# First B and C of a chunked scan: rows of 2048 bytes, turned on VectorE

## The chip, the cores and the metric

The kernel runs on one core of one Trainium2 chip. The metric is the device time of one execution in microseconds (us): three runs of the kernel before gave 373.04, 373.81 and 375.49, median 373.81.

## The reference

A gated state-space scan is followed by a gated feed-forward network. With 4 batches, 8 heads, 768 positions, head size 32, state size 16:

```python
for c in range(nc):                       # chunks; state is carried
    L = np.exp(cum[:, :, :, None] - cum[:, :, None, :]) * causal
    M = np.einsum('bhin,bhjn->bhij', Cc, Bc) * L
    y[:, :, sl] = M @ xc + (Cc @ state) * np.exp(cum)
    state = decay_full * state + sum_j(decay_from_j * Bc_j (x) xc_j)
x = y.transpose(0, 2, 1, 3).reshape(3072, 256)
out = (sigmoid(x @ w_gate) * (x @ w_val)) @ w_out      # d_ff = 1536
```

B and C are `[4, 8, 768, 16]` in memory, so the 16 values of one position of one head are 64 contiguous bytes, and 32 positions in a row are 2048.

## The kernel before, in words

The sequence is cut in 6 chunks of 128 positions, and each chunk in two halves of 64. A *unit* is one chunk of one batch (4 units a chunk, worked in pairs). For a unit TensorE transposes B and C (tile `pt`), ScalarE copies them out (`bct`), TensorE multiplies them (`pcb`), VectorE weighs that with the decays (`m`, line 478; the decays are scans, lines 419 and 586), and TensorE multiplies with x and adds the state (lines 490, 497, 541 or 624). The finished 128 positions x 4 batches are 512 columns of the network: gate and value (`pg`, `pv`, twelve pieces f = 0 to 11), then the projection (`po`, lines 839 and 850).

Chunk 0 is special. Its "unit" holds the first 64 positions of two batches (units 0 and 1, *first pair*) or the second 64 (units 2 and 3, *late pair*). Its decays come from matmuls `pa` (line 580) and scans (586). Its network starts as soon as the first pair is done: pieces f = 0 to 3 are run in halves (line 714; first halves need the first pair's result in `xw`, second halves the late pair's). Weights of the network are loaded as 512 KB pieces `wr` and taken apart in place by a chain of five steps (lines 318, 323, 325, 329, 331: VectorE, ScalarE, VectorE, ScalarE, GpSimd).

The order on every engine is fixed before the run: `run()` plays all tasks against a table of costs and writes each engine's program in the order that results. `DUES` overrides the due times of single tasks, `FIRST` orders the first loads, and constants such as `free` say when an engine is taken to be free. A load occupies one of 8 completion lanes; the load eight places later waits for that one to land. All loads go through SyncE's queue.

`load_first` (line 271) brings chunk 0's B, C and x in two DMAs of 64 partitions for each half, with positions on partitions: rows of 64 bytes for B and C, 128 for x. `products` (377) has two transposes for a unit, then an eviction by three ScalarE instructions, then 8 matmuls. `first_results` (604), `first_outputs` (629) and `first_states` (638) finish a pair. `spread` (572) makes the decays. The clipping of the whole `a` (903), its running product (912) and their way through memory (924, 927, 283, 291) give the later chunks their decays.

Of the kernel before, what the change touches and what calls it, by code (L numbers as in the profile page):

```python
# [8 lines left out]
F32 = mybir.dt.float32  # L9
# [8 lines left out]
DUES = {  # L18
# [13 lines left out]
}  # L32
WARM = 3


FIRST = "b0 c0 w0 x0 w1 b1 c1 w2 x1 w3 r w4 w5 w6 w7 w8 w9"
LANES = 8
# [30 lines left out]
def tile_ssd_then_gated_ffn(  # L68
# [16 lines left out]
    P = 128  # L85
# [90 lines left out]
    def step(eng, cost, needs=(), makes=(), port=False, **buffers):  # L176

        return eng, cost, needs, makes, port, buffers

    def run():  # L180

        free = {"sp": 1.0, "pe": 1.2 + 1.7 * WARM, "act": 3.5, "dve": 6.0, "pool": 6.2, "none": 0.0}
        port_free = [0.0]
        dma_free = 0.0
        landed = [0.0] * LANES
# [65 lines left out]
    def pair_of(tag, c, b, shape):  # L251

        k = tag, c, b // 2
        if k not in got:
            got[k] = ld.tile([P, 2, H, shape], F32, tag=tag, name=f"{tag}{c}_{b // 2}", bufs=2)
        return got[k]
# [13 lines left out]

    def load_first(tag, src, late, n):
        t = pair_of(tag, 0, 2 * late, n)
        for i in range(2):
            nc.sync.dma_start(  # L274
                t[i * L2 : (i + 1) * L2].rearrange("p u h n -> p (u h) n"),
                src[late * L2 : (late + 1) * L2, 2 * i * H : 2 * (i + 1) * H],
            )

    def load_a(c, b):
# [89 lines left out]
    class Unit:  # L369
# [7 lines left out]
        def products(self):  # L377

            c, b, u = self.c, self.b, self.u
            needs = [("bc", u)] if c else [("bc", u), ("b0", u // 2)]  # L380
            if c:
                needs += [("bct", u - 1 if c > 1 else -1), ("cb", u - 4), ("cd", u - 4)]
            yield step("pe", 0.24 if c else 0.45, needs, [("tp", u)], y=1)
# [4 lines left out]
            yield step("act", 0.9 if c else 1.1, [], [("bct", u)], y=-1)  # L388
            if c:
                self.bct = wk.tile([P, 4, L], F32, tag="bct", name=f"bct{self.nm}", bufs=4)  # L390
            else:

                if ("bct", b // 2) not in got:
                    got["bct", b // 2] = hp.tile([P, 2, 4, L], F32, tag=f"h{5 + b // 2}", name=f"bct{self.nm}")
                self.bct = got["bct", b // 2][:, b % 2]
            if u > 1:
                nc.scalar.copy(self.bct[:, :2].rearrange("p k l -> p (k l)"), pt[:, : 2 * L])
            else:
                nc.scalar.copy(self.bct[:, 0], pt[:, :L])
# [169 lines left out]
    class FirstUnit(Unit):  # L569


        def spread(self):

            u = self.u
            yield step("pe", 1.0, [("a0",)], banks=1)
            pa = ps_mm.tile([P, 512], F32, tag="mm", name=f"pa{u}")
            rows = slice(32 * (u // 2), 32 * (u // 2) + 32)
            for i in range(2):
                b = 2 * i + u % 2
                nc.tensor.matmul(  # L580
                    pa[i * L2 : (i + 1) * L2], of_b2[rows, b : b + 1].broadcast_to([32, L2]),
                    apart[rows].rearrange("p h l -> p (h l)"), start=True, stop=True,
                )
# [45 lines left out]
    def first_outputs(late):  # L629

        for i in range(2):
            yield step("act", ACT_HALF, [("inter" if late else "y", 2 * late + 1)], [("xf", late)] if i else [])
# [3 lines left out]
            nc.scalar.copy(out, got["py", late][:, i, :, 0])  # L636

# [307 lines left out]
    def initial():  # L945
# [16 lines left out]
    }  # L962
    for late in range(2):
        for tag, src, n, needs, makes in (
            ("b", b4, N, [], [("b0", late)]),
            ("c", c4, N, [], [("bc", 2 * late), ("bc", 2 * late + 1)]),
            ("x", x4, D, [], [("xn", 2 * late), ("xn", 2 * late + 1)]),
        ):
            loads[f"{tag}{late}"] = load(
                2, 1.9 if tag == "x" else 1.5, needs, makes, lambda a=(f"{tag}n", src, late, n): load_first(*a)  # L970
            )
    for i in range(NW):
# [8 lines left out]
    def unit(due, c, b):  # L981
# [9 lines left out]
        if c or b > 1:  # L991
            task(due, f"before{u.nm}", u.before())
        task(due - (0.0 if c else 30.0), f"products{u.nm}", u.products())
        task(due, f"decays{u.nm}", u.decays())
        if c == 0 and b % 2:
            task(due, f"result{u.nm}", first_results(pair.pop(), u))
            task(due, f"outputs{u.nm}", first_outputs(b // 2))
# [71 lines left out]
```

## Time and profile before

| what | us |
|---|---|
| runs shown, median (lowest to highest) | 373.81 (373.04 to 375.49) |
| the profiled execution, its own time | 374.85 |
| span of its trace | 373.0 |
| TensorE busy in the span | 360.9 (97%) |
| VectorE, ScalarE, GpSimd busy | 157.0, 151.1, 150.1 |
| TensorE busy in the first 31.62 | 24.89 |

In the trace PE is TensorE's matmuls, DVE VectorE, ACT ScalarE, POOL GpSimd, SPq the DMA issues of SyncE. [...] An idle time stands in brackets with what ended it; `issue` means that nothing in the profile shows what the engine waited for.

### The profile page before, as it was taken

What the parts mean: (1) busy time and instruction counts of PE and PEld (TensorE: products, weight loads), DVE (VectorE), ACT (ScalarE), POOL (GpSimd) and SP (SyncE); (2) the same over time, 40 slices, a digit from 0 to 9 for tenths busy, and PEclk for the clock granted to TensorE, in tenths of its full rate; (3) what the DMA queues carried; (4) which work ended last, traced back from release to release, by engine and by line L of the source; (5) the groups of instructions that cost most, each with busy time, mean ns of one, the idle gap of its engine ahead of it and who ended that gap; (6) DMA issues with size and microseconds to landing.
All of it is one profiled execution on the core that took longest, in us unless ns stands there. A gap on an engine that the chain in (4) does not pass through costs nothing.

```text
span 373.0 us, 8123 instructions
## 1 busy us (share of the span) xinstructions
PE 360.9 (97%) x3376; PEld 287.0 (77%) x3376; DVE 157.0 (42%) x277; ACT 151.1 (41%) x314; POOL 150.1 (40%) x159
## 2 busy tenths in 40 slices
PE   7788999999999999999999999999999999999996
PEld 2267668877878888888878888788877788888885
DVE  4756557768435444553354622430224440222201
ACT  2656686423575411544511245430254420254400
POOL 4425476463797520244440045430144420145410
PEclk9669999999999999999999999999999999999999
DMA  6999996527236322502332300400000000000000
GB/s 121 208 233 184 243 314 169 96 44 122 67 30 113 30 71 60 106 22 34 26 99 82 89 4 6 53 10 29 30 1 2 2 2 28 30 0 0 2 28 28
DMA packets 89270, 26.27 MB, mean 70 GB/s; under 512 B 76306, under 2 KB 82002, under 8 KB 89234
## 3 DMA queue, kind: packets, MB, share of 16 engines
q1 hardware_dynamic: 89234, 25.76, 31.8%
q8 instruction: 26, 0.43, 0.5%
q14 instruction: 10, 0.08, 0.1%
HBM read 22.41 MB, written 3.34 MB: 69 GB/s over the span
## 4 chain that ended last, share of the span: by engine, by line
PE 88%; SPq 5%; DMA 4%; POOL 1%; issue 1%; DVE 0%; ACT 0%
PE pv L813 25%; PE pg L813 24%; PE po L850 15%; PE po L851 7%; PE po L839 6%; DMA cn<-in_C_dram 2%; SPq L304 2%; PE pcb L464 2%; PE pcb L490 2%; PE pcb L541 2%; SPq L262 1%; DMA bn<-in_B_dram 1%; SPq L274 1%; PE pcb L497 1%; POOL wr L331 1%; PE pt L386 1%
## 5 line engine op out<-in xcount | busy, mean ns | idle before, releaser
L781 POOL TENSOR_TENSOR h<-g,h 128x512 fp32r<-128x512 f32 x60 | 78.5, 1308 | 126.6 <-ACT h L779 126.3
L813 PE MATMUL pv<-xh,w 128*128 128x512 f32 x264 | 93.9, 396 | 0.0
L813 PE MATMUL pg<-xh,w 128*128 128x512 f32 x264 | 93.3, 394 | 0.0
L850 PE MATMUL po<-w,h 128*128 128x512 f32 x228 | 82.1, 402 | 0.0
L775 DVE TENSOR_TENSOR g<-pv,g 128x512 f32<-128x512 f32 x60 | 41.5, 691 | 93.0 <-PE pv L813 87.5
L779 ACT CAST h<-g 128x512 fp32r<-128x512 f32 x59 | 36.6, 621 | 75.7 <-DVE g L775 75.7
L851 PE MATMUL po<-w,h 128*128 128x256 f32 x228 | 63.9, 280 | 0.0
L813 PEld LDWEIGHTS pg<-xh,w 128*128 128x128 f32 x264 | 49.6, 188 | 10.8 <-issue 0.2
L813 PEld LDWEIGHTS pv<-xh,w 128*128 128x128 f32 x264 | 49.6, 188 | 10.7 <-issue 0.3
L813 PE MATMUL pv<-xl,w 128*128 128x512 f32 x132 | 51.5, 390 | 0.0
L813 PE MATMUL pg<-xl,w 128*128 128x512 f32 x132 | 51.4, 390 | 0.0
L850 PEld LDWEIGHTS po<-w,h 128*128 128x128 f32 x228 | 42.8, 188 | 11.0 <-issue 0.5
L754 ACT ACTIVATE g<-pg 128x512 f32<-128x512 f32 x68 | 40.7, 599 | 14.7 <-PE pg L813 13.8
L851 PEld LDWEIGHTS po<-w,h 128*128 128x128 f32 x228 | 43.0, 189 | 0.2
L866 ACT COPY o<-po 128x256 f32<-128x256 f32 x20 | 7.5, 373 | 65.7 <-PE po L851 65.1
L419 DVE TENSOR_TENSOR_SCAN ab<-ab,delta 128x512 f32<-128x512 f32 x20 | 28.0, 1406 | 8.3 <-DMA ab<-a_z 8.2
L868 DVE TENSOR_TENSOR o<-po,o 128x256 f32<-128x256 f32 x20 | 8.4, 424 | 49.6 <-ACT o L866 49.5
L813 PEld LDWEIGHTS pg<-xl,w 128*128 128x128 f32 x132 | 24.8, 188 | 4.8
L813 PEld LDWEIGHTS pv<-xl,w 128*128 128x128 f32 x132 | 24.8, 188 | 4.6
L348 POOL TENSOR_TENSOR w<-wr,w 128x512 fp32r<-128x512 f32 x18 | 23.8, 1326 | 9.7 <-ACT w L346 8.8
L331 POOL TENSOR_TENSOR wr<-wr 128x512 int32<-128x512 int32 x18 | 19.6, 1091 | 20.0 <-ACT wr L329 17.9
L839 PE MATMUL po<-wr,h 128*128 128x256 f32 x96 | 23.4, 393 | 0.0
(96 smaller groups left out, 371.1 us busy)
## 6 DMA issues: line engine op xcount, KB each, us to landing
ab<-a_z SPq DMA_DIRECT2D x40, 128.0 KB
wr<-in_moe_w_val_dram SPq DMA_DIRECT2D x6, 512.0 KB
wr<-in_moe_w_gate_dram SPq DMA_DIRECT2D x6, 512.0 KB
wr<-in_moe_w_out_dram SPq DMA_DIRECT2D x6, 512.0 KB
out_dram<-o SPq DMA_DIRECT2D x24, 128.0 KB
xn<-in_x_dram SPq DMA_DIRECT2D x10, 256.0 KB
bn<-in_B_dram SPq DMA_DIRECT2D x10, 128.0 KB
cn<-in_C_dram SPq DMA_DIRECT2D x10, 128.0 KB
```

The source lines that it names most:

```text
L331: nc.gpsimd.tensor_tensor(out=lw.bitcast(I32), in0=hw.bitcast(I32), in1=lw.bitcast(I32), op=ALU.add)
L348: engines[eng].tensor_tensor(out=lo, in0=lw, in1=hi.bitcast(F32), op=ALU.subtract)
L419: nc.vector.tensor_tensor_scan(out=t.rearrange("p h l -> p (h l)"), data0=t.rearrange("p h l -> p (h l)"), data1=delta.rearrange("p h l -> ...
L754: nc.scalar.activation(gs[k, f], pm, AF.Sigmoid)
L775: nc.vector.tensor_tensor(out=g, in0=pm, in1=g, op=ALU.mult)
L779: copies[eng](hh, g)
L781: engines[eng].tensor_tensor(out=hl, in0=g, in1=hh.bitcast(F32), op=ALU.subtract)
L813: nc.tensor.matmul(pm, w[:, part, kt, fs], xx[:, kt], start=(i == 0), stop=(i == 3 * NK - 1))
L839: nc.tensor.matmul(acc[:, :DM], hs[k, f][:, js], whole[NF + f // 2][:, f % 2], start=start, stop=stop, skip_group_check=True,)
L850: nc.tensor.matmul(acc, hh, w.rearrange("p i m -> p (i m)"), start=start, stop=False, skip_group_check=True)
L851: nc.tensor.matmul(acc[:, :DM], hl, w[:, 0, :], start=False, stop=stop, skip_group_check=True)
L868: nc.vector.tensor_tensor(out=o, in0=acc[:, DM:], in1=o, op=ALU.add)
```

## The change

Five things are different in the program:

1. B and C of chunk 0 come as `rows`: 32 partitions x 2048 bytes in each of 4 DMAs (line 289 of the new kernel), and one VectorE instruction for each of B and C (line 297, `STREAM_TRANSPOSE`, 128x512) turns blocks of 32 by 32 so that positions lie on partitions as before.
2. C's rows and the first half of x are issued by ScalarE, ahead of its table load; the rest stays on SyncE.
3. `first_pair` takes the place of `products` in chunk 0: four transposes into one tile, one eviction of three wider instructions for both units, then 8 matmuls for each unit.
4. The `pa` matmuls and scans of units 2 and 3 wait for the first pair (`("cb", 1)`, `("mult", 1)`), and the second copy of `first_outputs` may go to VectorE.
5. `DUES`, `FIRST` and the start times in `free` have other numbers, which moves work of all stages.

```diff
-FIRST = "b0 c0 w0 x0 w1 b1 c1 w2 x1 w3 r w4 w5 w6 w7 w8 w9"
+FIRST = "b0 w0 w1 x1 w2 w3 r w4 w5 w6 w7 w8 w9"
+TURN = 0.6
...
-        free = {"sp": 1.0, "pe": 1.2 + 1.7 * WARM, "act": 3.5, "dve": 6.0, "pool": 6.2, "none": 0.0}
+        free = {"sp": 1.0, "pe": 0.6 + 1.7 * WARM, "act": 5.4, "dve": 5.4, "pool": 6.3, "none": 0.0}
...
+    def load_rows(queue, j):
+        if "rows" not in got:
+            got["rows"] = hp.tile([P, 2, 32, N], F32, tag="s0", name="rows")
+        src = (Bm, Cm)[j].rearrange("(i u) h (c o q t) n -> i c q (u h) o (t n)", u=2, o=2, q=2, t=32)
+        for i in range(2):
+            for q in range(2):
+                p = i * L2 + q * 32
+                queue.dma_start(got["rows"][p : p + 32, j].rearrange("p t n -> p (t n)"), src[i, 0, q])
+    def turn(j):
...
+        nc.vector.transpose(
+            got[tag].rearrange("p o u h n -> p n (u h) o"), got["rows"][:, j].rearrange("p t n -> p n t"),
+        )
...
+    def first_pair(*two):
...
+        for k in range(2):
+            for j, tag in enumerate(("bn", "cn")):
+                at = (2 * k + j) * L
+                nc.tensor.transpose(pt[:, at : at + L], got[tag, 0, late][:, k].rearrange("p h n -> p (h n)"), eye)
...
+        nc.scalar.copy(bct[:, :, :many], from_pt[:, :, :many])
+        for g in range(NG):
+            nc.scalar.mul(bct[:, :, 2 + g], from_pt[:, :, 1], of_g[:, g : g + 1])
...
-            yield step("pe", 1.0, [("a0",)], banks=1)
+            yield step("pe", 1.0, [("cb", 1)] if u > 1 else [("a0",)], banks=1)
...
-            yield step("dve", 1.22, [], [("scan", u)], banks=-1)
+            yield step("dve", 1.22, [("mult", 1)] if u > 1 else [], [("scan", u)], banks=-1)
...
+    load_rows(nc.scalar, 1)
+    load_first(nc.scalar, 0)
     nc.scalar.activation(table, table, AF.Sigmoid)
```

**The first loads.** SyncE's rows before (`cn_0`, `bn_0`: C and B of the first half; `cn_1`, `bn_1`: of the second; `DMAHW` is a completion lane):

```order
L883 DMA a_109<-in_a_dram 64x1x128
L274 DMA cn_0_121<-in_C_dram 64x16x16 x2
L304 DMA wr_124<-in_moe_w_val_dram 128x2x512
L274 DMA bn_0_126<-in_B_dram 64x16x16 x2
L304 DMA wr_129<-in_moe_w_val_dram 128x2x512
L274 DMA cn_1_131<-in_C_dram 64x16x16
L274 DMA cn_1_131<-in_C_dram 64x16x16 [waits DMAHW0_49]
```

and SyncE's now:

```order
L917 DMA a_109<-in_a_dram 64x1x128
L326 DMA wr_129<-in_moe_w_gate_dram 128x2x512
L289 DMA rows<-in_B_dram 32x1x512 x2
L289 DMA rows<-in_B_dram 32x1x512 [waits DMAHW1_49]
L289 DMA rows<-in_B_dram 32x1x512 [waits DMAHW2_49]
L326 DMA wr_135<-in_moe_w_val_dram 128x2x512 [waits DMAHW4_49]
```

B's third piece waits for lane 1, which is that of `a`, and its fourth for lane 2, which is that of the first weight. C's four pieces and x are ScalarE's.

**VectorE ahead of the first weighing** (`m_0`, `m_1` of the first pair), now:

```order
L340 TENSOR_SCALAR wr_129<-wr_129 128x512 [waits DMAHW2_49]
L297 STREAM_TRANSPOSE cn<-rows 128x16x16x2 [waits DMAHW4_49,DMAHW6_49,DMAHW3_49,DMAHW0_49]
L297 STREAM_TRANSPOSE bn<-rows 128x16x16x2 [waits DMAHW5_49,DMAHW7_49,DMAHW2_49,DMAHW1_49]
L704 SCALAR_TENSOR_TENSOR ap_161<-early 32x64 [waits Pool_49]
L592 SCALAR_TENSOR_TENSOR ab_0_163<-pa_144,delta 128x512 [waits PE_49]
L340 TENSOR_SCALAR wr_135<-wr_135 128x512 [waits DMAHW4_49]
L592 SCALAR_TENSOR_TENSOR ab_1_182<-pa_156,delta 128x512 [waits PE_49]
L340 TENSOR_SCALAR wr_137<-wr_137 128x512 [waits DMAHW5_49]
L340 TENSOR_SCALAR wr_139<-wr_139 128x512 [waits DMAHW6_49]
L347 TENSOR_SCALAR wr_135<-wt_188 128x512 [waits Activation_49]
L484 TENSOR_TENSOR m_0_225<-pcb_0_190,ab_0_163 128x512 [waits PE_49]
```

Before, all four scans stood ahead of `m_0`; now two do, and the two turns and more weight steps.

**TensorE around the late pair.** Before (`pg_f_i`, `pv_f_i`: piece f, half i of the network; lines 490 and 497 are the pair's products):

```order
L714 MATMUL pv_1_0_368<-xw_308,wr_124 128x256
L490 MATMUL pcb_2_330<-m_2_354,xn_1_222 32x64 [waits DMAHW3_49,DVE_49]
...
L624 MATMUL pcb_2_330<-cd_3_317,m_0_312 64x64 x4
L714 MATMUL pg_2_0_462<-xw_308,wr_203 128x256 [waits DMAHW1_49,Pool_49]
L714 MATMUL pg_2_0_462<-xw_308,wr_203 128x256
L714 MATMUL pv_2_0_471<-xw_308,wr_129 128x256 [waits DMAHW6_49,DVE_49]
L714 MATMUL pv_2_0_471<-xw_308,wr_129 128x256
L714 MATMUL pg_3_0_482<-xw_308,wr_203 128x256 [waits DVE_49]
L714 MATMUL pg_3_0_482<-xw_308,wr_203 128x256
```

and now:

```order
L748 MATMUL pg_2_0_376<-xw_303,wr_129 128x256 [waits DMAHW2_49,DVE_49,Pool_49]
L748 MATMUL pg_2_0_376<-xw_303,wr_129 128x256
L748 MATMUL pv_2_0_381<-xw_303,wr_152 128x256 [waits DMAHW1_49,Activation_49,Pool_49]
L748 MATMUL pv_2_0_381<-xw_303,wr_152 128x256
L496 MATMUL pcb_1_326<-m_2_344,xn 32x64 [waits DMAHW2_49]
...
L655 MATMUL pcb_1_326<-cd_3_296,m_0_308 64x64 x4
L748 MATMUL pg_3_0_472<-xw_303,wr_129 128x256 [waits Activation_49]
L748 MATMUL pg_3_0_472<-xw_303,wr_129 128x256
```

`pg_2_0` and `pv_2_0` have moved from behind the late pair to ahead of it; `pg_3_0` now follows the pair directly.

## Rows read from the trace of the kernel before

**Rows 1.** The page: queue of instruction DMA (packets, MB, share of 16 engines).

```profile
q8 instruction: 26, 0.43, 0.5%
```

**Rows 2.** Busy time by stretch (start:end, engines with instruction counts, clock, DMA share, GB/s).

```profile
0.00:31.62 31.62, 24.89 (x346) 14.06 (x346) 18.12 (x43) 15.00 (x35) 12.01 (x23) 0.78 0.89 197
27.45:29.20 1.75, 1.75 (x130) 1.59 (x129) 0.53 (x2) 0.78 (x2) 1.04 (x1) 1.00 1.02 393
60.00:370.00 310.00, 309.74 (x2897) 253.74 (x2895) 122.93 (x208) 114.77 (x235) 119.11 (x118) 1.00 0.21 43
```

**Rows 3.** The same view by half microseconds.

```profile
3.50:4.00 0.50, 0.50 (x2) 0.18 (x1) 0.00 (x0) 0.00 (x0) 0.00 (x0) 1.00 1.10 103
11.00:11.50 0.50, 0.50 (x8) 0.23 (x4) 0.50 (x1) 0.00 (x0) 0.50 (x1) 0.96 1.01 55
25.00:25.50 0.50, 0.50 (x4) 0.45 (x3) 0.21 (x2) 0.00 (x0) 0.32 (x1) 0.88 0.21 29
```

**Rows 4.** Timeline of PE (start, duration, records; idle time before and its end).

```profile
11.47 1.97 PE L580 MATMUL pa<-apart,of_b 32*64 32x512 f32 x4
15.85 0.45 PE L386 MATMUL pt<-eye,bn 128*128 128x128 f32 x1 [1.58 <-DMA bn<-in_B_dram]
18.12 0.68 PE L490 MATMUL pcb<-m,xn 64*32 64x64 f32 x32
21.18 2.05 PE L714 MATMUL pg<-xw,wr 128*128 128x256 f32 x4 [1.44 <-issue]
29.20 1.14 PE L714 MATMUL pg<-xw,wr 128*128 128x256 f32 x4
31.04 0.59 PE L714 MATMUL pg<-xw,wr 128*128 128x256 f32 x2
33.12 0.71 PE L714 MATMUL pg<-xw,wr 128*128 128x256 f32 x2 [1.50 <-issue]
45.98 0.33 PE L387 MATMUL pt<-eye,cn 128*128 128x128 f32 x1 [0.61 <-DMA cn<-in_C_dram]
70.99 0.46 PE L490 MATMUL pcb<-m,xn 64*32 64x64 f32 x32
```

**Rows 5.** Timeline of SyncE's DMA issues.

```profile
0.74 0.71 SPq L883 DMA_DIRECT2D a<-in_a_dram  x1
2.93 0.71 SPq L304 DMA_DIRECT2D wr<-in_moe_w_val_dram  x1
50.41 0.41 SPq L927 DMA_DIRECT2D a_p<-a  x1
```

**Rows 6.** Timeline of DVE.

```profile
4.30 0.22 DVE L889 TENSOR_SCALAR ac<-a 64x128 f32<-64x128 f32 x1 [2.04 <-DMA a<-in_a_dram]
7.61 0.43 DVE L318 TENSOR_SCALAR wr<-wr 128x512 f32<-128x512 f32 x1 [2.25 <-DMA wr<-in_moe_w_val_dram]
15.04 1.22 DVE L586 TENSOR_TENSOR_SCAN ab<-pa,delta 128x512 f32<-128x512 f32 x1
17.30 0.68 DVE L478 TENSOR_TENSOR m<-pcb,ab 128x512 f32<-128x512 f32 x1
42.41 1.74 DVE L912 TENSOR_TENSOR_SCAN a<-a,a 32x768 f32<-32x768 f32 x1
54.55 0.68 DVE L771 TENSOR_TENSOR h<-pv,g 128x512 f32<-128x512 f32 x1
67.00 0.69 DVE L478 TENSOR_TENSOR m<-pcb,ab 128x512 f32<-128x512 f32 x1
```

**Rows 7.** Timeline of ACT.

```profile
16.55 0.37 ACT L397 COPY bct<-pt 128x256 f32<-128x256 f32 x1 [0.69 <-PE pt L387]
```

**Rows 8.** DMA view, instruction packets in windows 22.4 to 23.9, 30.3 to 31.6, 34.5 to 35.6.

```profile
q8 instruction: 1, 0.02, 5.7%
q8 instruction: 1, 0.02, 5.9%
q8 instruction: 1, 0.02, 5.2%
```

More of the change, by code (lines that the diff above doesn't have):

```diff
@@ L254, in pair_of @@
         if k not in got:
-            got[k] = ld.tile([P, 2, H, shape], F32, tag=tag, name=f"{tag}{c}_{b // 2}", bufs=2)
+            if tag not in got:
+                got[tag] = ld.tile([P, 2, 2, H, shape], F32, tag=tag, name=tag, bufs=1)
+            got[k] = got[tag][:, b // 2]
         return got[k]
@@ L269, in load_x, with load_first @@
         nc.sync.dma_start(t[:, bs].rearrange("p b h d -> p (b h) d"), x4[cs, hs])
-    def load_first(tag, src, late, n):
-        t = pair_of(tag, 0, 2 * late, n)
+    def load_first(queue, late):
+        t = pair_of("xn", 0, 2 * late, D)
         for i in range(2):
-            nc.sync.dma_start(
+            queue.dma_start(
                 t[i * L2 : (i + 1) * L2].rearrange("p u h n -> p (u h) n"),
-                src[late * L2 : (late + 1) * L2, 2 * i * H : 2 * (i + 1) * H],
+                x4[late * L2 : (late + 1) * L2, 2 * i * H : 2 * (i + 1) * H],
             )
+    def load_rows(queue, j):
[7 more added lines that the diff above has]
+    def turn(j):
+        yield step("dve", TURN, [("rows", j)], [("b0", 0), ("b0", 1)] if j == 0 else [("bc", u) for u in range(NB)])
+        tag = ("bn", "cn")[j]
+        for late in range(2):
+            pair_of(tag, 0, 2 * late, N)
+        nc.vector.transpose(
+            got[tag].rearrange("p o u h n -> p n (u h) o"), got["rows"][:, j].rearrange("p t n -> p n t"),
+        )
     def load_a(c, b):
@@ L379, in products @@
             c, b, u = self.c, self.b, self.u
[L380 to L383, printed above, removed]
+            needs = [("bc", u), ("bct", u - 1 if c > 1 else -1), ("cb", u - 4), ("cd", u - 4)]
+            yield step("pe", 0.24, needs, [("tp", u)], y=1)
             bn, cn = (got[k, c, b // 2][:, b % 2].rearrange("p h n -> p (h n)") for k in ("bn", "cn"))
@@ L387, in products @@
             nc.tensor.transpose(pt[:, L : 2 * L], cn, eye)
[L388 to L399, printed above, removed]
+            yield step("act", 0.9, [], [("bct", u)], y=-1)
+            self.bct = wk.tile([P, 4, L], F32, tag="bct", name=f"bct{self.nm}", bufs=4)
+            nc.scalar.copy(self.bct[:, :2].rearrange("p k l -> p (k l)"), pt[:, : 2 * L])
             for g in range(NG):
@@ L602, in decays @@
             yield from self.decayed()
+    def first_pair(*two):
+        us, late = [t.u for t in two], two[0].u // 2
+        yield step("pe", 0.8, [k for u in us for k in (("bc", u), ("b0", late))], [("tp", u) for u in us], y=1)
+        pt = ps_y.tile([P, 512], F32, tag="py", name=f"pt0_{late}")
+        for k in range(2):
+            for j, tag in enumerate(("bn", "cn")):
+                at = (2 * k + j) * L
+                nc.tensor.transpose(pt[:, at : at + L], got[tag, 0, late][:, k].rearrange("p h n -> p (h n)"), eye)
+        yield step("act", 1.5 if late else 1.15, [], [("bct", u) for u in us], y=-1)
+        bct = hp.tile([P, 2, 4, L], F32, tag=f"h{5 + late}", name=f"bct0_{late}")
+        from_pt = pt.rearrange("p (u k l) -> p u k l", u=2, k=2)
+        many = 2 if late else 1
+        nc.scalar.copy(bct[:, :, :many], from_pt[:, :, :many])
+        for g in range(NG):
+            nc.scalar.mul(bct[:, :, 2 + g], from_pt[:, :, 1], of_g[:, g : g + 1])
+        for k, t in enumerate(two):
+            t.bct = bct[:, k]
+            units[t.u] = t
+        for k, (t, u) in enumerate(zip(two, us)):
+            yield step("pe", 0.3, [], [("cb", u)], **({} if k else {"cb": 1}))
+            if k == 0:
+                pcb = ps_cb.tile([P, NQ, 512], F32, tag="pcb", name=f"pcb0_{late}")
+            multiply(pcb, k, t)
     def first_results(*two):
@@ L631, in first_outputs @@
         for i in range(2):
-            yield step("act", ACT_HALF, [("inter" if late else "y", 2 * late + 1)], [("xf", late)] if i else [])
+            eng = yield step(
+                ("act", "dve") if i else "act", (ACT_HALF, DVE_HALF) if i else ACT_HALF,
+                [("inter" if late else "y", 2 * late + 1)], [("xf", late)] if i else [],
+            )
             if not xw:
@@ L635, in first_outputs @@
             out = xw[0].rearrange("p k (i u s l) -> p k i u s l", i=2, u=2, s=2)[:, :, i, :, late]
-            nc.scalar.copy(out, got["py", late][:, i, :, 0])
+            copies[eng](out, got["py", late][:, i, :, 0])
     def first_states(late):
@@ L953, in initial @@
         yield step("none", 4.9, [], [("a0",)])
+        yield step("none", 0.3, [], [("rows", 1)])
+        yield step("none", 2.8, [], [("xn", 0), ("xn", 1)])
     task(-60.0, "", initial())
@@ L962, in tile_ssd_then_gated_ffn @@
     }
[L963 to L971, printed above, removed]
+    loads["x1"] = load(2, 1.9, [], [("xn", 2), ("xn", 3)], lambda: load_first(nc.sync, 1))
+    loads["b0"] = load(4, 0.9, [], [("rows", 0)], lambda: load_rows(nc.sync, 0))
+    task(-9.5, "turn0", turn(0))
+    task(-9.4, "turn1", turn(1))
     for i in range(NW):
@@ L992, in unit @@
             task(due, f"before{u.nm}", u.before())
-        task(due - (0.0 if c else 30.0), f"products{u.nm}", u.products())
+        if c:
+            task(due, f"products{u.nm}", u.products())
         task(due, f"decays{u.nm}", u.decays())
         if c == 0 and b % 2:
+            task(due - 30.0, f"products{u.nm}", first_pair(pair[-1], u))
             task(due, f"result{u.nm}", first_results(pair.pop(), u))
```

9 lines of the change are left out of this document (2 added, 7 removed), and 25 rows, old and new, of the table DUES.

## The prediction

> **What bounds the kernel now.** I read the windows first, to find where TensorE is not full. From 60 to 370 us it is busy for 309.74 of 310.00 [rows 2], so what the change does there can only cost. Nothing but the way to a full TensorE can be shortened: in the first 31.62 us it is busy for 24.89, with 346 matmul records [rows 2], and the clock is at half in part of that [rows 3]. Next I read TensorE's timeline for the idle times that remain. Four count. At 15.85 it has waited 1.58 for B's second half; at 21.18, where the network begins, 1.44 for the first pair's result; at 33.12 it has waited 1.50 in the middle of `pg_3_0`, for nothing that a semaphore shows; at 45.98 it has waited 0.61 for C of chunk 1 [rows 4]. [...]
>
> The wait at 33.12 needs a word. TensorE had issued the first of two equal matmuls and stood before the second, which waits for nothing new. The profile has one queue of instruction packets, 26 of them [rows 1]; one lies in 30.3 to 31.6 and others in 22.4 to 23.9 and 34.5 to 35.6 [rows 8]. 3376 matmuls over 26 packets are 130 for a packet, and the late pair alone runs 130 records in 1.75 us [rows 2]. So I read this wait as TensorE running out of program: the late pair uses up one packet so fast that the next is late. This is an inference; it carries the forecast.
>
> The profiled execution took 374.85, 1.04 above the median of 373.81; I sum differences inside it and set them against the median.
>
> **First loads.** Removed are eight loads with 64-byte rows, which ran at 103 GB/s with all DMA engines busy [rows 3]. Added are eight of 2048 bytes. B is now the later of the two: its fourth piece waits until the first weight has landed. That weight took from 2.93 to 7.61 [rows 5, 6], 4.7 us, behind 64-byte rows; issued at 1.5 it lands at 6.2 by that row, or at 5.0 if the 1.2 us of 128 KB at 103 GB/s falls away. A small load takes 3.6 from issue to use (`a`, 0.74 to 4.30) [rows 5, 6]. B is whole between 8.6 and 9.8. I take 8.6, since nothing with short rows stands ahead of the weight. ScalarE's six issues and its table load end long before its first copy, and cost nothing.
>
> **The turns.** No row shows a `STREAM_TRANSPOSE`. The same 128x512 is 0.43 as one-operand work and 1.22 as a scan [rows 6]; I take 0.68, the plain two-operand row, which is nearest to one pass over one value at a time. C's turn lies before B has landed and is free; B's is on the path: VectorE is ready at 9.3, TensorE begins the four transposes there.
>
> **First pair.** VectorE's row behind the turns: `ap` (0.3), two scans (2 x 1.22), three clamps and a shift (4 x 0.43), `m_0` (0.68), two weight steps (0.86), `m_1` (0.68) [rows 6]: 6.7, so `m_1` is done at 16.0; before, it was done at 17.98. TensorE: transposes to 10.0; ScalarE's three evictions of 256 columns at 0.37 [rows 7], some 1.0, to 11.0; first products about 0.7 (32 such small records took 0.68 at half clock), four transposes about 1.3 (one takes 0.45 at half clock, and they overlap), second products 0.7, overlapping a little, to 13.4; then two `pa` at half clock, 1.97 each with some 0.2 overlapped [rows 4], to 17.1. Both engines count, TensorE is later by 1.1. x, now behind C alone and not behind two weights, has landed by then. The pair's products begin at about 16.9 in place of 18.12, and the same 3.06 (18.12 to 21.18) follow up to `pg_0_0` [rows 4]: **20.0 in place of 21.18**. With the late end for B it is 21.2, with the turn at its dear end 0.5 later still, with the cheap ends 19.5.
>
> **The clock.** [...] If the clock comes back at 25.0 again, 1.2 us gained at half rate are worth 0.6; if it comes back 3.82 after the start of the big matmuls as before (21.18 to 25.0) [rows 3, 4], 1.2. I take 0.9. [...]
>
> **The late pair.** It began at 27.45. Now `pg_2_0` and `pv_2_0` stand ahead of it, 1.84 (29.20 to 31.04) [rows 4]: 27.45 - 0.9 + 1.84 = 28.4. It runs 1.75 [rows 2], and half of `pg_3_0` takes 0.59, so TensorE stands before the second half at 30.7; before it stood there at 31.62, so 0.9 is gained so far. By the rows of the program it has then run the same 346 records. If the packet is asked for at a place in the program, it comes a fixed time after the late pair's start: 33.12 - 27.45 = 5.7 as it was; at the light end 4.0, from the third packet, which was in by 35.6, 2.5 after TensorE went on, if it is usable 1.5 after that, as the second was (in by 31.6, used at 33.12) [rows 4, 8]. That gives 32.4 to 34.1; the middle, since loads are about as dense there as before, is 33.2. **The cover that is gone** is the 1.84 of `pg_2_0` and `pv_2_0`: the gain of 0.9 turns into a longer wait, and the stage ends 0.1 later than before.
>
> **Behind it.** The wait of 0.61 for C of chunk 1 goes, since two of the chunk's transposes now come after piece 6. The weights of the network come in another order with output weights between them; the DMA engines have saved 512 KB of 64-byte rows, some 4 us, so I cost that at nothing. TensorE's work is the same. Sum: +0.1 - 0.6 = -0.5 on the profiled execution, about **373.2** on the median's scale. Ends of the forecast, from B, the clock and the packet: 372.0 to 374.5.
>
> **The rivals.**
>
> *The packet is not late* (or the 1.50 was something else). For it: no semaphore proves my reading, and `pg_3_0` is the only such place. Against it: the packet lies inside the wait's approach, 30.3 to 31.6 [rows 8]. Then TensorE goes on at 30.7, 2.4 sooner than 33.12, and with the 0.6 the time is 370.8. [...]
>
> [...]
>
> *The packet is later still*, the slower end. The loads now run without a pause from the start, eight lanes deep. If the packet's wait is that of the first one (asked for in the first pair's products at about 18.4 at the latest, in at 23.9, usable 1.5 later: 7.0), TensorE goes on at 35.4, 2.3 later than before; less 0.6, the time is 375.5. It decides from a wait of 5.3 after the late pair's start.
>
> *The decays of chunk 1 come late*. The scan of `a` ended at 44.15; now it stands behind piece 6's product, which began at 54.55, and SyncE's save at 50.41 and all decay loads stand behind the scan [rows 5, 6]. The save slips by 2 to 6 us. The second weighing was ready at 67.69; TensorE took the pair at 70.99 [rows 4, 6] and now has one more group of projection first, so some 5 us of slack. Beyond that, up to 1.5 is lost: 374.7, and more if a weight is late with it.
>
> **How the numbers follow.** Chances: forecast 0.40, packet not late 0.23, that with the clock 0.08, packet later 0.18, decays or weights late 0.11. The likeliest gives 373.2. The range leaves out the clock rival, part of "the packet is not late" below 369.7, and the worst of the last two above 375.8. A measurement tells about 1%, 3.7 us: faster than 370.07 is the clock rival and a third of "not late", 0.15; slower than 377.55 only the tail of the last two, 0.05; within, 0.80.
>
> **What would show it.** In the profile after: C's turn before B's last row, each turn near 0.68; first pair's products at about 17; `pg_0_0` near 20; half clock up to about 25; a wait of 2 to 3 us with the releaser "issue" in `pg_3_0`, behind an instruction packet, ending near 33; no wait for C of chunk 1. If `pg_3_0` runs through, the first rival was right. If TensorE waits on VectorE's weighing near 70, the decays were late. The forecast is wrong altogether if TensorE is not full from 46 on.

## The result, and the profile after

In one comparison on one chip the kernel before took 373.57 us (median of 20 executions) and the changed kernel 375.04 (20): ratio 1.0042, interval 1.0030 to 1.0054. The change makes the kernel slower, by 1.5 us, where 373.2 was forecast. The time lies inside the range (369.7 to 375.8), beyond the ends given for the forecast itself (372.0 to 374.5), and on the wrong side of the kernel before. The profiled executions tell another story than the medians: 374.56 (span 372.8) after, against 374.85 (span 373.0) before. The execution that I had read of before was one of its long ones; that of after is one of its short ones.

The first lines are TensorE's timeline of the changed kernel (start, duration, records, idle time before and its end). They answer to [rows 4].

```profile
5.97 1.93 PE L586 MATMUL pa<-apart,of_b 32*64 32x512 f32 x8
9.80 0.45 PE L618 MATMUL pt<-eye,bn 128*128 128x128 f32 x1 [1.90 <-DVE ap L704]
10.82 1.22 PE L715 MATMUL pp<-early 32*128 32x256 f32 x2
14.29 3.62 PE L586 MATMUL pa<-apart,of_b 32*64 32x512 f32 x8
17.84 0.68 PE L496 MATMUL pcb<-m,xn 64*32 64x64 f32 x32
20.79 2.05 PE L748 MATMUL pg<-xw,wr 128*128 128x256 f32 x4 [1.33 <-issue]
29.66 0.45 PE L496 MATMUL pcb<-m,xn 64*32 64x64 f32 x32
31.38 1.14 PE L748 MATMUL pg<-xw,wr 128*128 128x256 f32 x4
34.15 1.02 PE L748 MATMUL pv<-xw,wr 128*128 128x256 f32 x4 [1.63 <-issue]
```

The network starts at 20.79 in place of 21.18, a gain of 0.4 and not of 1.2. `pg_3_0` (31.38) now runs through, and the wait that nothing explains has moved one piece on, to `pv_3_0`: 1.63, until 34.15. In the profile of before `pv_3_0` started at 33.67. Behind it no wait is left, that for C of chunk 1 included. So in the two profiles the change loses 0.5 at `pv_3_0` and wins 0.7 behind it, 0.6 of that the wait for C of chunk 1.

The next are VectorE's rows; they answer to [rows 6].

```profile
3.82 0.22 DVE L925 TENSOR_SCALAR ac<-a 64x128 f32<-64x128 f32 x1 [1.56 <-DMA a<-in_a_dram]
5.90 0.47 DVE L340 TENSOR_SCALAR wr<-wr 128x512 f32<-128x512 f32 x1 [1.03 <-DMA wr<-in_moe_w_gate_dram]
7.69 1.06 DVE L297 STREAM_TRANSPOSE cn<-rows 128x512 f32<-128x512 f32 x1 [1.32 <-DMA xn<-in_x_dram]
8.65 1.01 DVE L297 STREAM_TRANSPOSE bn<-rows 128x512 f32<-128x512 f32 x1
9.56 0.23 DVE L704 TENSOR_TENSOR_SCAN ap<-early 32x64 f32<-32x64 f32 x1
15.97 0.69 DVE L484 TENSOR_TENSOR m<-pcb,ab 128x512 f32<-128x512 f32 x1
```

VectorE's first weight step starts at 5.90 (7.61 before), but a turn costs 1.0 and not 0.68, and C's turn, which I had counted as free, runs directly ahead of B's.

Then the windows (start:end, length, busy PE, PEld, DVE, ACT, POOL, clock, DMA share, GB/s), which answer to [rows 2, 3]:

```profile
0.00:31.62 31.62, 27.25 (x345) 15.03 (x346) 20.24 (x43) 13.46 (x27) 13.18 (x24) 0.73 0.92 278
8.50:9.00 0.50, 0.00 (x0) 0.00 (x0) 0.50 (x2) 0.00 (x0) 0.00 (x0) 0.78 0.97 243
9.80:20.79 10.99, 9.61 (x146) 4.83 (x147) 8.42 (x14) 6.78 (x16) 5.04 (x8) 0.50 1.08 325
25.50:26.00 0.50, 0.50 (x17) 0.27 (x17) 0.00 (x0) 0.00 (x0) 0.00 (x0) 0.65 1.05 389
46.00:60.00 14.00, 14.00 (x86) 9.85 (x86) 9.68 (x12) 9.91 (x21) 12.16 (x11) 1.00 0.24 50
```

The granted clock falls from 1.00 to 0.50 near 8.7 (0.78 in 8.50 to 9.00), while TensorE idles for the turns (1.90, up to 9.80), and is back near 25.8 (0.65 in 25.50 to 26.00); in the profile of before it was away from 11.4 to 25.0. In the same 31.62 us TensorE is busy for 27.25 in place of 24.89, for the same records: it is denser, but at a mean clock of 0.73 in place of 0.78.

### The profile page after: what moved, and what is told of

The parts are those of the page before. It is cut to its first block, busy times and chain, and to the rows that moved or that the text cites. A ratio compares the mean times of both kernels' runs of the same rounds, so it can differ in the third digit from the quotient of the medians.

```text
span 372.8 us, 8119 instructions
## 1 busy us (share of the span) xinstructions
PE 363.5 (98%) x3376; PEld 287.9 (77%) x3376; DVE 160.1 (43%) x278; ACT 150.1 (40%) x309; POOL 152.3 (41%) x159
## 4 chain that ended last, share of the span: by engine, by line
PE 95%; DMA 2%; issue 1%; DVE 1%; ACT 0%; SPq 0%; DVEq 0%
PE pg L847 25%; PE pv L847 24%; PE po L884 15%; PE po L885 7%; PE po L873 6%; PE pcb L496 2%; PE pcb L470 2%; PE pv L748 2%; PE pg L748 2%; PE pcb L547 2%; PE pcb L503 1%; DMA wr<-in_moe_w_gate_dram 1%; PE pg L838 1%; PE pv L838 1%; PE pa L586 1%; PE pt L406 1%
## 5 line engine op out<-in xcount | busy, mean ns | idle before, releaser
L847 PE MATMUL pg<-xh,w 128*128 128x512 f32 x264 | 94.8, 400 | 0.0
L353 POOL TENSOR_TENSOR wr<-wr 128x512 int32<-128x512 int32 x18 | 22.0, 1230 | 18.6 <-ACT wr L351 13.6
L425 DVE TENSOR_TENSOR_SCAN ab<-ab,delta 128x512 f32<-128x512 f32 x20 | 25.4, 1273 | 5.1 <-DMA ab<-a_z 4.8
```

Source lines behind the costliest of these rows:

```text
L353: nc.gpsimd.tensor_tensor(out=lw.bitcast(I32), in0=hw.bitcast(I32), in1=lw.bitcast(I32), op=ALU.add)
L425: nc.vector.tensor_tensor_scan(out=t.rearrange("p h l -> p (h l)"), data0=t.rearrange("p h l -> p (h l)"), data1=delta.rearrange("p h l -> ...
L847: nc.tensor.matmul(pm, w[:, part, kt, fs], xx[:, kt], start=(i == 0), stop=(i == 3 * NK - 1))
```

## The experiments

Two readings of the loss stood against each other at first. **Packet**: the wait in the middle of the network is the load of TensorE's next program packet; typical executions of before hardly have it, those of after always do. **Clock**: the change costs TensorE more time at half clock. A *record* is one matmul in the profile, and a *boundary* the record at which TensorE is taken to need the next packet. Ratios are to the kernel before, run on the same chip in the same comparison.

### Before and after again (e1, e2, e8)

No edit.

> The kernel before, unchanged, to see typical executions of it with their spans and clocks beside the profiled one (374.85, mean clock 0.982). Theory 'packet': what differs between its executions is the wait of 1.50 us in pg_3_0; most runs are then near 373.5 with the mean clock 0.982 unchanged, and a profile of such a run has no wait, or one shorter by 1 us or more, before the second half of pg_3_0, or has it at the same length where the run is 374.5 or more. Theory 'clock': what differs is how long TensorE runs at half clock; a typical run has a mean clock above 0.982 (0.984 to 0.987), and its profile shows half the clock for 10 to 12 us in place of 13.65 and the same 1.5 us wait.

> The changed kernel, unchanged. Both theories: 1.0042 times the kernel before, 374.6 to 375.3. 'Packet': its wait of 1.63 us before pv_3_0 is there in every profile. 'Clock': half clock for 17 us, mean clock 0.977, in every profile.

> The changed kernel, unchanged, beside the two below on the same chip, and for one more profile of it. 'Packet': 1.6 us of wait before pv_3_0 again, 374.3 to 375.3 where nothing else is late; an execution of 376 or more has a further wait or a longer one, with the clock as in the others. 'Loads' makes no other forecast here.

Before: 373.92 (ratio 0.9992, 0.9982 to 1.0003). After: 374.85 (1.0025, 1.0009 to 1.0042) and 375.02 (1.0033, 1.0014 to 1.0053). Of the 42 timed executions of after most lie between 374.1 and 375.8, and 11 at 375.9 to 376.4. TensorE in the second profile of before (374.08):

```profile
21.56 2.05 PE L714 MATMUL pg<-xw,wr 128*128 128x256 f32 x4 [1.44 <-issue]
28.89 0.45 PE L490 MATMUL pcb<-m,xn 64*32 64x64 f32 x32
32.48 1.41 PE L714 MATMUL pg<-xw,wr 128*128 128x256 f32 x4
33.73 1.03 PE L714 MATMUL pv<-xw,wr 128*128 128x256 f32 x4
```

`pg_3_0` shows no wait in this one, but it takes 1.41 where a piece directly behind another takes 1.03: the third of its four records comes 0.3 late, near 33.18 (an estimate: 33.73 less the 0.55 from that record to `pv_3_0` in the first profile, 33.12 to 33.67). The half clock lasted until 27.7 here (0.85 in 27.5 to 28.0), in place of 25.0 in the first profile; TensorE came to `pg_3_0` 1.4 later, and `pv_3_0` started at 33.73, against 33.67. So **clock** falls: mean clock 0.977 here, as in after, and what the clock gives back ahead of the packet the wait takes. **Packet** stands, though its forecast had the mean clock at 0.982 here. In after the wait was 1.59 in e2 (`pv_3_0` at 34.49) and 0.81 in e8 (33.79), where 1.6 was forecast.

### The gap ahead of the transposes filled (e3)

```diff
+            if u == 1:
+                for i in range(2):
+                    nc.tensor.matmul(
+                        warm.rearrange("p (r l) -> p r l", r=4), warm_sb,
+                        warm_sb.rearrange("p (r l) -> p r l", r=1).broadcast_to([P, 4, P]), start=True, stop=True,
+                    )
```

> The changed kernel with two more 128x512 matmuls of zeros ahead of the first transposes, in the 1.90 us in which TensorE waits for VectorE's turns (7.90 to 9.80). Nothing else moves. Theory 'clock': the loss is the clock that falls at 8.7, 2.7 us earlier than before, because TensorE is idle there; with the gap filled it falls at 11 to 12, the mean clock is 0.980 to 0.983 and the time 0.6 to 1.4 below that of the changed kernel, near 373.9. Theory 'packet': the two instructions hardly move the place in the program, the wait before pv_3_0 comes at a fixed time of the late pair, and the time stays within 0.4 of the changed kernel.

376.46 (1.0059, 1.0040 to 1.0078): slower, against both forecasts. Three of the six executions lie at 375.6 to 375.9 and three at 377.1 to 377.3; the profile is of the longest. The clock did stay up, to 17 (1.00 in 12.5 to 16.0), but the first pair then waited 1.74 for VectorE's weighing and began at 17.45, only 0.4 sooner; the clock fell in that wait (0.50 in 17.5 to 27.0) and was away until 27.5. The four records more moved the unexplained wait one piece up, to before `pg_3_0`, now 2.05 long, and behind it the clock fell once more (0.50 in 34.5 to 37.0). That the wait goes with the record count and not with a piece speaks for **packet**.

### The cover put back, the cover taken away (e4, e7)

The first puts `pg_2_0` and `pv_2_0` of the changed kernel behind the late pair, the second puts those of the kernel before ahead of it.

```diff
+        if (f, i) == (2, 0):
+            before += [("inter", 3)]
```

> The changed kernel with pg_2_0 and pv_2_0 behind the late pair again, as in the kernel before; the order of later work moves with them, where TensorE is full. Theory 'packet': the wait of 1.63 us is covered by the 1.84 us of these two pieces, TensorE goes on 1.0 to 1.6 us earlier, time 373.5 to 374.1 (0.996 to 0.998 of the changed kernel). Theory 'clock': half clock lasts as long as in the changed kernel (17 us), and the time stays near 375.0.

```diff
+        if late:
+            needs.append(("pv", 0, 2, 0))
```

> The kernel before with pg_2_0 and pv_2_0 ahead of the late pair, as in the changed kernel, and nothing else on purpose (the order of later work moves a little with it). 'Packet': the block between two boundaries is now the late pair alone, TensorE runs it in 1.8 us and then waits 2.0 to 2.8 us in or behind pg_3_0 in place of 0 to 1.5; it goes on at 33.8 to 35.3 in place of 33.1 to 33.4; time 0.6 to 2.0 above the kernel before. 'Loads': the packet is used at 33.2 as before, the time stays within 0.3.

381.50 (1.0195, 1.0173 to 1.0216) and 378.54 (1.0110, 1.0085 to 1.0135). Both miss: the edits moved more than they were meant to. In e4 the pair began at 27.12, 2.5 sooner, and yet TensorE stood before `pv_3_0` until 33.70:

```profile
33.29 0.62 ACT L762 ACTIVATE g<-pg 128x256 f32<-128x256 f32 x2
33.69 0.74 PEld L748 LDWEIGHTS pv<-xw,wr 128*128 128x128 f32 x4 [2.38 <-ACT g L762]
33.70 1.16 PE L748 MATMUL pv<-xw,wr 128*128 128x256 f32 x4 [1.99 <-ACT g L762]
47.40 0.33 PE L407 MATMUL pt<-eye,cn 128*128 128x128 f32 x1 [1.16 <-DMA cn<-in_C_dram]
```

By the trace this wait is one for ScalarE and not for the packet: the two sigmoids run from 33.29 for 0.62, and the weight load (PEld) ahead of the first matmul of `pv_3_0`, which in after ran at 32.14, before the wait, ran at 33.69 here. Its packet, begun in 30.3 to 31.8, took 1.4. So e4 does not test the packet. Behind 33.70 it loses 6.4 against after, to the clock behind the wait (0.50 in 35 to 37) and to waits for chunk 1. In e7 `pg_2_0` waited 1.28 for a weight that was not taken apart yet; it does not test the packet.

### The packet boundary moved (e5, e6, e9)

32 (e5, e6) or 16 (e9) small matmuls of zeros behind the second `pa` move every boundary 64 or 32 records towards the start; nothing else changes place.

```diff
+            got["pas"] = got.get("pas", 0) + 1
+            if got["pas"] == 2:
+                for i in range(32):
+                    nc.tensor.matmul(warm[:32, :32], warm_sb[:32, :32], warm_sb[:32, :32], start=True, stop=True)
```

> The changed kernel with 32 small matmuls of zeros (32x32, 64 records) ahead of the first transposes, in TensorE's idle time before 9.8. They move every packet boundary 64 records towards the start of the work: the one before pv_3_0 (record 348) goes to the middle of the late pair, and the block behind it then holds half the late pair and 18 us of the network. Theory 'packet' (a packet is asked for where TensorE enters the one before it, and is usable 4.5 us after that at the earliest; the late pair runs through a block in 3 us): no wait before pv_3_0 or anywhere else in 24 to 46, TensorE goes on at 32.5 in place of 34.2, time 1.2 to 1.8 below the changed kernel, 373.2 to 373.8. Rival 'loads' (the packet waits behind the burst of weight loads until 31.2 wherever the boundary lies, and so does something else that TensorE needs): a wait of 1 us or more stays, ending near 34, time within 0.4 of the changed kernel.

> The kernel before with the same 64 records ahead of its first transposes. 'Packet': the boundary in pg_3_0 (record 346) goes to the middle of the late pair. Executions that had no wait there (as the one of the second profile, where TensorE came to it at 33.1) gain 0 to 0.3; those that came early and waited 1.5 gain up to that, unless the wait for C of chunk 1 grows by as much: 0.995 to 1.000 of the kernel before, 372.2 to 373.9. 'Loads': as the kernel before within 0.3.

> The changed kernel with 16 in place of 32 small matmuls, 32 records, some 1.3 us, which fit the idle time ahead of the first transposes. The boundary of pv_3_0 goes 32 records up, into the last third of the late pair; the block in front of it begins at pv_0_0 or pg_1_0 and takes TensorE 7 us. 'Packet': no wait in 24 to 46, and no 1.2 us lost at the start as with 32: pg_0_0 at 20.8, pv_3_0 at 32.5 to 32.8, time 0.7 to 1.1 below that with 32 matmuls, 372.7 to 373.2. Rival: what TensorE comes earlier is lost to another wait (C of chunk 1, a weight, ScalarE's sigmoid) before 60, as in the kernel before with the shift, and the time is that with 32 matmuls within 0.3.

After with 32: 373.92 (0.9988, 0.9973 to 1.0003), none of 12 above 374.7. Before with 32: 374.91 (1.0003, 0.9984 to 1.0021). After with 16: 373.32 (0.9989, 0.9974 to 1.0004). TensorE in e5:

```profile
22.02 2.05 PE L752 MATMUL pg<-xw,wr 128*128 128x256 f32 x4 [1.33 <-issue]
32.60 1.14 PE L752 MATMUL pg<-xw,wr 128*128 128x256 f32 x4
33.58 1.03 PE L752 MATMUL pv<-xw,wr 128*128 128x256 f32 x4
```

The network starts 1.2 later than in after, and `pv_3_0` 0.6 sooner, with no wait. A kernel with useless work added is faster (0.9988 against 1.0025 to 1.0042 without), by this reading because its packets are cut elsewhere. **Packet** forecast this (with 373.2 to 373.8 a little more of it), **loads** did not. Before with the shift also loses its wait (`pv_3_0` at 32.88), but not its time, where **packet** had left room for up to 1.5 and **loads** forecast none: 0.41 of a wait for ScalarE at 54.33 is seen, and its profile (span 372.4) stands where that of e1 does (372.3). These runs together say most about the cause: moving the boundary takes after from 1.0025 to 1.0042 down to 0.9988 and 0.9989, and leaves before at 1.0003. With 16 in place of 32 the time should have been 0.7 to 1.1 lower; by the ratios it is the same, as the rival had it. In the one profile of e9, of its longest execution (375.24), a weight landed late: `wr` of `pv_2` stands between the two copies of `xw` on ScalarE.

```profile
19.27 0.37 ACT L674 COPY xw<-pcb 128x256 f32<-128x256 f32 x1 [0.82 <-PE pcb L503]
20.85 0.67 ACT L345 ACTIVATE wt<-wr 128x512 f32<-128x512 f32 x1 [1.21 <-DVE wr L340]
21.42 0.36 ACT L674 COPY xw<-pcb 128x256 f32<-128x256 f32 x1
```

### The clock kept up (e10)

```diff
+            if got["pas"] == 2:
+                fill(warm, 512)
+                for i in range(16):
+                    nc.tensor.matmul(warm[:32, :32], warm_sb[:32, :32], warm_sb[:32, :32], start=True, stop=True)
+            if got["pas"] == 4:
+                got["fill"] = ps_y.tile([P, 512], F32, tag="py", name="fill")
+                fill(got["fill"], 512, 256)
...
+            fill(got["fill"], 512, 128)
```

> The changed kernel with matmuls of zeros in three idle times of TensorE: 128x512 and 16 small ones ahead of the first transposes, 128x512 and 128x256 ahead of the first pair's products, 128x512 and 128x128 behind them; 44 records more ahead of the network, so no packet is late. [...] Rival: the clock falls all the same near 15 to 17, the fillers delay the pair, and the time is 373.5 to 375; or what comes earlier is lost to weights that are late, time 373 to 374.

374.13 (1.0004, 0.9986 to 1.0022), where 371 to 372 was forecast for a clock that stays full up to the network. The whole network ran at full clock (1.00 in 23 to 46), but it began at 23.06 in place of 20.79: the second filling waited for ScalarE until 17.35 and then ran for 2.93 at a clock that had fallen (0.57 in 17 to 22), ahead of the pair. What the clock gains the filling loses: `pv_3_0` at 33.28, and 374.13 is some 2 above that forecast.

### The weight from between the copies (e11, e12)

Both copies of the first pair's result are written at the first one's place. e11 is after with this alone, e12 has the 16 small matmuls as well.

```diff
+            for j in ([i] if late else [[0, 1], []][i]):
...
-            copies[eng](out, got["py", late][:, i, :, 0])
+                copies[eng](out, got["py", late][:, j, :, 0])
```

> The changed kernel with the two ScalarE copies of the first pair's result (xw) next to each other; the clamp of the weight wr_152, which the change had put between them, comes behind both. Nothing else moves. Theory 'weight between': the executions of the changed kernel at 376 and above are those in which that weight lands 1 us or more late (VectorE's step on it waits for its load; in one profile it came at 20.3 in place of 18.3) and holds the second copy and the network; with the copies together none lies above 375.5, the network starts 0.3 to 0.6 earlier, the wait for the packet stays (1.5 to 1.8 us before pv_3_0), and the median goes from 375.0 to 374.0 to 374.6. Rival: those executions have a longer wait for the packet, or something behind 34; then a quarter of them still lie near 376.

> The same with the 16 small matmuls (32 records) ahead of the first transposes as well. 'Packet' and 'weight between' together: no wait in 24 to 46 and no execution above 374.5; pg_0_0 at 20.2 to 20.8, pv_3_0 at 32.0 to 32.8, median 372.2 to 373.0, below both the kernel before (by 0.2 to 0.4%) and the changed kernel. Rival: what comes earlier is lost behind 34 (C of chunk 1, a weight), 373.2 to 373.6.

e11: 375.23 (1.0019, 0.9999 to 1.0038). The network starts at 20.21, 0.6 sooner than in after, and all of it goes into the wait, 1.91, `pv_3_0` at 34.25. Four of twelve still lie at 376.1 to 376.8, so a late weight is not what makes these. e12: **373.23, ratio 0.9971 (0.9958 to 0.9983)**, none of 10 above 374.1: below the kernel before and the changed one. The ratio is the one forecast; the time lies at the lower end of the rival's. The same 0.6 now reaches `pv_3_0`; against e9 (0.9989, on another chip) the two intervals still overlap.

```profile
20.09 2.05 PE L753 MATMUL pg<-xw,wr 128*128 128x256 f32 x4 [0.78 <-POOL bd L435]
31.40 1.14 PE L753 MATMUL pg<-xw,wr 128*128 128x256 f32 x4
32.38 1.03 PE L753 MATMUL pv<-xw,wr 128*128 128x256 f32 x4
```

From `pv_3_0` to the end of the span it is 338.7 here and 338.6 in e1, e5 and after. What decides between these profiles is when TensorE gets there. (In e9 and e6 it is 339.3 and 339.6.)

### What the executions near 376 are (e13 to e16)

e13 puts two 128x512 matmuls of zeros where TensorE would wait; the others are after (e14, e15) and e11 (e16), unchanged, for one profile each.

```diff
+        to = ps_y.tile([P, 512], F32, tag="py", name="fill")
+        for n in range(2):
+            nc.tensor.matmul(
+                to.rearrange("p (r l) -> p r l", r=4), warm_sb,
+                warm_sb.rearrange("p (r l) -> p r l", r=1).broadcast_to([P, 4, P]), start=True, stop=True,
+            )
```

> The changed kernel with two 128x512 matmuls of zeros between the late pair and pg_3_0, 1.7 us of useless work where TensorE would wait for its program; the boundary comes 4 records earlier, in front of pg_3_0. Theory 'clock behind the wait' (in the executions at 376 TensorE's clock falls to half in or behind the wait, and 3.4 us at half rate lose 1.7): with TensorE busy up to 32.6 the wait that is left is below 0.6 before pg_3_0, and pg_3_0 starts near 33.2; time of the shorter executions 374.8 to 375.8 (the useless work is in place of the wait, and pg_3_0 comes behind it), but none lies 1.3 us or more above the median. Theory 'packet later still in these executions': a quarter to a third lie 1.5 above the rest, as without the filling.

> The changed kernel, unchanged, for the profile of an execution near 376. 'Clock behind the wait': if its time is 375.8 or more, a stretch at half clock lies behind the wait before pv_3_0 (34 to 38) and pv_3_0 does not start later than 34.6; if it is below 375.4, there is no such stretch. 'Packet later still': at 375.8 or more pv_3_0 starts at 35.5 or later, with the full clock behind it.

> The same again: 'clock behind the wait' and 'packet later still' as for the look before.

> The changed kernel with the two copies of xw together, whose executions lay near 376 four times in twelve: 'clock behind the wait' and 'packet later still' as for the looks before, with a wait of 1.9 us or more before pv_3_0.

e14 came at 376.14, e15 at 374.58, e16 at 374.61. TensorE and its windows in e14:

```profile
33.95 1.02 PE L748 MATMUL pv<-xw,wr 128*128 128x256 f32 x4 [1.98 <-issue]
36.24 1.92 PE L748 MATMUL pv<-xw,wr 128*128 128x256 f32 x4
```

```profile
34.50:35.00 0.50, 0.50 (x4) 0.46 (x3) 0.00 (x0) 0.18 (x1) 0.17 (x1) 1.00 1.28 122
35.00:38.00 3.00, 3.00 (x9) 2.36 (x9) 1.29 (x4) 1.46 (x3) 1.29 (x1) 0.51 0.83 203
38.50:41.00 2.50, 2.50 (x14) 2.23 (x13) 1.41 (x4) 0.95 (x2) 2.42 (x3) 1.00 1.08 363
```

`pv_3_0` starts at 33.95, no later than in the short executions (33.79 to 34.49); then TensorE works at half clock from 35.0 to near 38.5, a `pv` takes 1.92 in place of 1.03, and that loses the 1.7. e15 (wait 1.30) and e16 (1.63) have no such stretch. **Clock behind the wait** holds in the one long execution of after that a profile caught. In e13, 375.58 (1.0048, 1.0034 to 1.0062), all five executions lie at 374.8 to 375.7, as forecast, but five are few where a quarter was to be long. A wait of 1.45 was left, not 0.6, since the pair began 0.9 sooner in its profile and TensorE still went on only at 33.95.

### Before once more (e17, e18)

No edit.

> The kernel before, unchanged. Theory: an execution near 373.5 has no wait in pg_3_0 above 0.5 us and none for C of chunk 1, and pv_3_0 starts at 33.0 to 33.4, where the two profiles so far had 33.67 and 33.73. Rival: pv_3_0 starts at 33.7 as in those, and what is shorter lies behind it.

> The same again: below 373.7 the theory has pv_3_0 at 33.0 to 33.4; at 374 or more it has pv_3_0 at 33.7 or a wait for C of chunk 1, and at 375.3 or more a stretch at half clock behind a wait in pg_3_0.

Both fell on long executions, 376.34 and 376.67, and neither shows the one near 373.5 that I wanted. But they show the packet at work in the kernel before. TensorE in e17, then in e18:

```profile
30.95 0.59 PE L714 MATMUL pg<-xw,wr 128*128 128x256 f32 x2
33.79 0.71 PE L714 MATMUL pg<-xw,wr 128*128 128x256 f32 x2 [2.24 <-issue]
34.33 1.53 PE L714 MATMUL pv<-xw,wr 128*128 128x256 f32 x4
35.66 1.91 PE L714 MATMUL pg<-xw,wr 128*128 128x256 f32 x4
```

```profile
28.89 0.45 PE L490 MATMUL pcb<-m,xn 64*32 64x64 f32 x32
32.48 0.59 PE L714 MATMUL pg<-xw,wr 128*128 128x256 f32 x2
35.13 0.71 PE L714 MATMUL pg<-xw,wr 128*128 128x256 f32 x2 [2.06 <-issue]
35.68 1.03 PE L714 MATMUL pv<-xw,wr 128*128 128x256 f32 x4
```

In e17 the clock falls behind the wait (0.50 in 35 to 38). In e18 it does not, though the forecast had it so at 375.3 or more: there the late packet alone makes the time.

e18 and e1 are the same program and reach `pg_3_0` at the same 32.48; one waits 2.06 there, the other 0.3. The loads ahead of it differ. The window 30 to 32 in e1, then in e18 with its packet, which is begun in 31.9 to 33.6 (in 30.3 to 31.8 in e1):

```profile
30.00:32.00 2.00, 2.00 (x46) 1.82 (x39) 1.22 (x5) 0.65 (x2) 0.19 (x1) 1.00 1.04 113
```

```profile
30.00:32.00 2.00, 2.00 (x46) 1.81 (x39) 1.22 (x5) 0.64 (x2) 0.19 (x1) 1.00 1.23 260
q8 instruction: 1, 0.02, 5.6%
```

In e18 the weights still run at 260 GB/s where in e1 they are nearly through (113), and its packet is begun later. That the packet comes behind the burst of loads is argued from these two; no run changed the loads alone.

In the fourteen profiles in which TensorE waits at a boundary near the late pair (before, after, e1 to e3, e7, e8, e11 and e13 to e18) it goes on at 33.1 to 35.1, while the pair starts anywhere from 27.1 to 31.6. In the five with the boundary moved (e5, e6, e9, e10, e12) TensorE does not wait there. The last step shows in two profiles. In before the packet begun in 30.3 to 31.6 has landed by 31.7, and TensorE goes on at 33.12, 1.4 later. In after it is the one packet begun in 31.2 to 32.6; it lands at 32.57, and TensorE goes on at 34.15, 1.6 later:

```profile
q8 instruction: 1, 0.02, 5.6%
```

## Why the prediction was wrong, step by step

- **The step that failed** is the last of the sum: "+0.1 - 0.6 = -0.5 on the profiled execution, about 373.2 on the median's scale". Inside the profiles it nearly holds: 0.5 is lost at `pv_3_0` (forecast 0.1), 0.7 won behind it (0.6), and the time is 0.3 less. What failed is carrying that over to the medians. I had noted that the execution was 1.04 above the median, and took that for a constant offset. The profile of before lies 1.28 above the median of its 20 executions, that of after 0.48 below its own; these 1.76 turn -0.3 into +1.5. Both terms hang on two waits, 1.50 and 0.61. The second belonged to that execution and not to the kernel: e1 has none, and is 0.7 shorter with `pv_3_0` at the same place. For the first this is not shown by a profile. e1 waits 0.3, but had come there 1.4 later; e17 and e18 wait 2.24 and 2.06. That a median execution of before pays little for it is taken from e6, where moving the boundary gains nothing.
- **The packet** was the right mechanism by the runs with the boundary moved (no wait there in e5, e6, e9, e10 and e12), and "the cover that is gone" the right reason. Its time was wrong. The late pair's step let it come "a fixed time after the late pair's start", 5.7 or at the light end 4.0. From that start until TensorE goes on it took 5.7, 4.3 (e1), 6.7 (e17) and 6.2 (e18) in before, and 4.5, 4.4 (e2), 3.7 (e8), 4.9 (e14) and 4.2 (e15) in after. In after TensorE has only `pg_3_0` behind the pair, and stands at the boundary 0.8 to 2.0 before it can go on, each time. In before two more pieces cover the time, and e1, with the pair at 28.9, waits 0.3. So on the median's scale the change seems to add this wait, where the forecast let it lengthen one.
- **The clock**: the term of 0.9 was worth nothing, and in e1 against the first profile a clock that came back 2.6 later cost nothing at `pv_3_0` (33.73 against 33.67): by this reading the packet sets the time either way. The chance of 0.08 was for a clock that stays up in a denser start. In after it did not (0.73 in the first 31.62 us); with the gap ahead of the transposes filled it was 1.00 in 12.5 to 16.0 and fell behind that (e3). What I left out is the clock behind a long wait: 11 of 42 executions of after lie at 375.9 or more, and the one profiled (e14) lost 1.7 so.
- **The turns**: 1.06 and 1.01, forecast 0.68; the bound (up to 1.22) held. C's turn was not free: it began only at 7.69, behind a wait that the profile puts down to x's load, and then stood directly ahead of B's. A turn took 1.0 for 512 elements a lane, with this strided output, where one-operand work of the same size takes 0.43 [rows 6].
- **First pair**: `m_1` was done at 16.7 (forecast 16.0), the products began at 17.84 (16.9) and the network at 20.79 (20.0). The step left out TensorE's `pp`, 1.22, and started the transposes 0.5 too early; its own terms also add up to 17.1 and not 16.9. **First loads** were right: the first weight was in by 5.90 (forecast 5.0 to 6.2), and B's turn ran at 8.65 without a wait for B (forecast 8.6).
- **Late pair** at 29.66, forecast 28.4: the 0.8 of `pg_0_0`, and the clock back at 25.8 in place of 25.0.
- **C of chunk 1**: the wait is gone, as said. **Decays of chunk 1**: not late; TensorE is full from 34.15 on.
- **The rivals**: "packet later still" gave 375.5, near the measured time, but that is luck: it had TensorE going on at 35.4, 7.0 after the pair's start, and it went on at 33.8 to 34.5, at most 4.9 after. "Packet not late" is nearly the case of e1 for the kernel before (0.3) and of no profile of after: 0.8 to 2.0 each time.

**Open**: the wait puts `pv_3_0` of after at 33.8 to 34.5. From 373.6 for the median of before, less 1.8 around the span and 338.6 behind `pv_3_0`, it would start there at 33.2 (an estimate); the earliest seen is 33.67. So half a microsecond of the 1.5 rests on an execution that no profile caught. What sets the time of the packet, and how much of it the loads do, is open too.

## What to carry to other kernels

A wait that one profile shows can belong to that execution: when its time lies above the median, ask first whether the wait is the difference, and take a second profile before summing. Where TensorE runs many small matmuls in a row, count records between program packets (some 130 here, from 3376 in 26), and keep slow work between the same two packets as these matmuls; 32 records more ahead of the late pair (e9, 0.9989) were worth more here than a network that starts 0.6 sooner (e11, 1.0019). Time won ahead of such a wait was worth nothing until the wait was gone: the same edit gave nothing in e11, and with the boundary moved (e12) the lowest ratio of all, if not clear of e9's.

## What the runs showed of the hardware

- After a program packet of 16 KB (0.43 MB in 26 packets) had landed, TensorE went on 1.4 us later in before (31.7, 33.12) and 1.6 in after (32.57, 34.15). In the executions of the two kernels without an edit it went on 3.7 (e8) to 6.7 us (e17) after the start of the late pair, and in the same program at 33.1 to 35.1 (before, e18). TensorE paid 0.3 (e1, e7) to 2.2 us (e17) for it, with the releaser "issue" or with another named (e8 and e15: VectorE's `sn`, which in after was over at 32.87, 1.3 before TensorE went on).
- After waits of 1.98, 1.99, 2.05 and 2.24 (e14, e4, e3, e17) the granted clock fell to 0.50 for a while, and a piece of four records took 1.9 in place of 1.03; after 1.63, 1.91 and once 2.06 (after, e11, e18) the pieces took 1.03.
- Full clock early did not last by itself: in e3 it was 1.00 in 12.5 to 16.0, and 0.50 in 17.5 to 27.0, behind a wait of 1.74 that ended at 17.45.
